# Attention's softmax division moved from each head pair to each finished token tile

## The chip, the core and the metric

The kernel runs on one core of one Trainium2 chip. A core has five engines that run their own queues in order and meet through semaphores: TensorE (PE, matmuls; PEld is its weight load), VectorE (DVE), ScalarE (ACT), GpSimd (POOL) and SyncE (SP, which here only issues DMAs). The metric is the time of one execution on the device in microseconds; lower is better.

## The reference, cut to what matters

Three stages follow each other: attention with a top-32 mask, a dense feed-forward layer ("MoE1" below) and a layer of 8 experts with top-1 routing.

```
scores = (1 / sqrt(64)) * q @ k^T              # 4 batches, 8 heads, 576 tokens, 64 per head
mask   = scores >= (32nd largest of the row)
attn   = exp(where(mask, scores, -1e9) - max)
attn   = attn / (sum(attn) + 1e-9)             # the division that the change moves
x      = (attn @ v), heads side by side         # 2304 tokens x 512
h = x @ w_in ; g = relu(h) + log1p(exp(-|h|)) ; x2 = g @ w_out      # MoE1, 2048 wide
out    = expert of argmax(x2 @ w_gate): relu(x2 @ w1[e]) @ w2[e], times its gate weight
```

## The kernel before

Attention works on groups. A group is two "tiles" of 128 query rows x 576 keys; there are 72 groups, and 80 products with the values, since the two heads of a pair share one product tile. For one group PE computes scores into PSUM (`emit_qk`, L387), ACT copies them to SBUF (L395), and DVE finds the 32 largest of each row: pairwise maxima and minima (L423 to L439), rounds of MAX8 and MATCH_REPLACE8 (L429 to L447). ACT takes the exponential (L436), DVE the mask (L458, with the product on POOL in L459, or L455 for both in one), ACT and POOL split the result into two float16 parts (L463 to L465), a DMA of SP's queue transposes it (L467, `pT`).

Three groups later (`LAG`) `emit_av` multiplies by the values. The value tile carries a column of ones, so column 64 of the PSUM tile `m` holds the sum of the exponentials (L482, L484). `m` has one buffer. Then, for each of the 80 head pairs, DVE forms the reciprocal of the two sums (L506, L508) and ACT writes each of the two heads, scaled by it, into the token tile `x` (L510). The next product cannot start before these two copies have read `m`.

A token tile (128 tokens x 512) is finished after four head pairs; there are 18. `unit_x` then splits it: ACT rounds it to float16 (`xh`, L529), POOL subtracts for the second part (L530), SP's queue transposes (L531, `xT`). One or two tiles make one of 10 units of MoE1; a unit is 16 steps, each of 12 matmuls with `w_in` (`layer1`, L569), four activations, an addition on POOL (L578) and, two steps later, the matmuls with `w_out` (`layer2`, L603; in the last two units L600). Then `route` writes the tile's rows and expert. In the first 300 us the weights of MoE1 are also decoded (L226 to L239). After attention and MoE1 comes the expert stage (`part_two`, L903 and L916 on PE).

What sets the order: the code emits groups, products and 1.7 steps of MoE1 per group with priorities (`A_SC`, `A_AV`, `AHEAD`), and a scheduler lays each engine's queue out from them and its own estimates. So an edit moves neighbours too. If a run's checks of magnitudes fail, a second, slower path (`flags is None`) does everything again; it is built but not executed here.

Of the kernel before, what the change touches and what calls it, by code (L numbers as in the profile page):

```python
# [8 lines left out]
F32 = mybir.dt.float32  # L9
# [4 lines left out]
AF = mybir.ActivationFunctionType  # L14
ALU = mybir.AluOpType
# [4 lines left out]
B, H, S, D = 4, 8, 576, 64  # L20
# [3 lines left out]
NP = H // 2  # L24
# [12 lines left out]
ESC = 1024.0  # L37
LN_ESC = 6.931471805599453
SCORE = 0.125
X_UP = 5  # L40
# [6 lines left out]
XB = 1  # L47
# [137 lines left out]
def part_one(tc, ctx, q, k, v, w_in, w_out, const, ident, before, ones, iota_e, reg_e, wg, ids,  # L185
             ohcum, done, early, table, rows, flags, sums, w_sums):
    nc = tc.nc
    late = []

    def pool(name, bufs, **kw):  # L190
        return ctx.enter_context(tc.tile_pool(name=name, bufs=bufs, **kw))
# [6 lines left out]
    xp = pool("xp", 1)  # L198
    wp = pool("wp", 1)
    sm = pool("sm", 4)  # L200
# [169 lines left out]
    sc_t, pt_t, o_t, x_t = {}, {}, {}, {}  # L370
# [98 lines left out]

    def x_tile(key):  # L470
        if key not in x_t:
            x_t[key] = xp.tile([128, NP, 2, D], F32, name=f"x{key[1]}", bufs=XB if isinstance(key[1], int) else 1)
        return x_t[key]

    def emit_av(m, kind):
        b, hp = pairs[m]
        v16, sc = pair[m][3:5]
        pT = pt_t.pop((m, kind))
        def products(o, pT, h):
            for r in range(R):  # L480
                c = r if r < 5 else r - 5
                nc.tensor.matmul(o[:, h, 0:D + 1], lhsT=pT(r), rhs=v16[:, h, c, 0:D + 1], start=r == 0, stop=r == R - 1)  # L482
                if r < 5:
                    nc.tensor.matmul(o[:, h, 0:D], lhsT=pT(r), rhs=v16[:, h, c, D + 2:], start=False, stop=False)  # L484

        def out_tile():
            return ps_m.tile([128, 512], F32, name="m")[:, :2 * D + 4].rearrange("p (h c) -> p h c", h=2)

        if kind == "tail":
            o = out_tile()  # L490
            p0 = 64 * (b % 2)
            for h in range(2):
                products(o[p0:p0 + 64], lambda r: pT[:, r, h * 64:h * 64 + 64], h)
            xt, ps_ = x_tile((b // 2, "tail%d" % (b // 2))), slice(p0, p0 + 64)
        else:
            t, h = kind
            if h == 0:
                o_t[m, t] = out_tile()
            o = o_t[m, t]
            products(o, lambda r: pT[:, r, :], h)  # L500
            if h == 0:
                return
            del o_t[m, t]
            xt, ps_ = x_tile((b, t)), slice(0, 128)
        rc = sm.tile([128, 2, 1], F32, name="rc")
        nc.vector.tensor_scalar(rc[ps_], o[ps_, :, D:D + 1], ESC * 1e-9,  # L506
                                2.0 ** -X_UP if flags is not None else sc[ps_, 2:3], op0=ALU.add, op1=ALU.mult)
        nc.vector.reciprocal(rc[ps_], rc[ps_])  # L508
        for h in range(2):
            nc.scalar.activation(xt[ps_, hp, h], o[ps_, h, 0:D], AF.Copy, scale=rc[ps_, h])  # L510


    def unit_x(tiles):
        n = 128 * len(tiles)
        up, dn, hs = 1.0, None, None
        if flags is None:
            bs = sorted({b for key, _ in tiles for b in ([key[0]] if isinstance(key[1], int) else [2 * key[0], 2 * key[0] + 1])})
            up = sm.tile([128, 1], F32, name="xup")
            nc.vector.tensor_reduce(up, v_up[:, bs[0]:bs[-1] + 1], op=ALU.min, axis=AX.X)
            dn = sm.tile([128, 1], F32, name="xdn")  # L520
            nc.vector.tensor_scalar(dn.bitcast(I32), up.bitcast(I32), -1.0, float(254 << 23), op0=ALU.mult, op1=ALU.add)
            hs = sm.tile([128, DFF // C], F32, name="hs")
        xT = xtp.tile([128, 2, 2, KD, 128], F16, name="xT")
        for i, (key, _) in enumerate(tiles):
            xv = x_t.pop(key).rearrange("p c h d -> p (c h d)")
            if flags is None:
                nc.scalar.activation(xv, xv, AF.Copy, scale=up)
            xh = x2p.tile([128, 2, DM], F16, name="xh", bufs=XHB)
            nc.scalar.activation(xh[:, 0], xv, AF.Copy)  # L529
            nc.gpsimd.tensor_tensor(out=xh[:, 1], in0=xv, in1=xh[:, 0], op=ALU.subtract)  # L530
            nc.sync.dma_start_transpose(out=xT[:, i].rearrange("p r c t -> p (r c) t"), in_=xh.rearrange("p r c -> p (r c)"))  # L531
        return xT, hs, dn

# [3 lines left out]
    def moe_step():  # L537

        if not cur and ready:
            cur.append(Unit(*ready.pop(0)))  # L540
        if cur:
            u = cur[0]
            if u.x is None:
                u.x = unit_x(u.tiles)
            layer1(u)
            behind.append((u, u.f))
            u.f += 1
            if u.f == KF - XAHEAD and ready:
                cur.append(Unit(*ready.pop(0)))
                cur[1].x = unit_x(cur[1].tiles)  # L550
            if u.f == KF:
                cur.pop(0)
        if behind and (not cur or len(behind) > GLAG):
            layer2(*behind.pop(0))
# [203 lines left out]
    for i in range(-1, n + LAG):  # L758
# [29 lines left out]
        if j >= 0:  # L788
            with tc.high_priority(offset=A_AV), ExitStack() as behind_scores:
                if i + 1 < n:  # L790

                    behind_scores.enter_context(tc.issue_after(last_qk[0].ins))
                for x in groups[j]:
                    emit_av(*x)
            for u in units.get(j, []):
                started += 1
                ready.append((u, started))
# [274 lines left out]
```

## Time and profile before

| what | value |
|---|---|
| median of 3 runs | 1112.18 us (1107.73 to 1112.3) |
| profiled execution | 1110.92 us |
| its span, first to last instruction | 1109.0 us |
| busy over the span | DVE 86%, PE 81%, ACT 72%, POOL 58% |

The span covers all but 1.92 us of the profiled execution. A share of busy time is a mean over stages: attention lasts to about 775 us (the last score copy starts at 757 us), what remains of MoE1 to about 870 us, and the expert stage to the end.

### The profile page before, as it was taken

To read this page: it belongs to the slowest core of one execution; us is meant where nothing else is said; L and a number is where in the kernel's file an instruction comes from. 1 tells how busy PE (TensorE), PEld (TensorE's weight loads), DVE (VectorE), ACT (ScalarE), POOL (GpSimd) and SP (SyncE) were. 2 spreads that over 40 slices of the span, in tenths; PEclk is the share of its full clock that TensorE was granted. 3 is DMA by queue.
4 is the path that set the end of the run, shared out by engine and by line. 5 is a ranking of instruction groups with operands and counts; after the bars stand their busy time and mean duration, and the time that the engine had idled before them with its cause. 6 is when DMAs were issued, how large, how long until landed. Compare 5 with 4: busy or idle time off the path is not lost.

```text
span 1109.0 us, 22601 instructions
## 1 busy us (share of the span) xinstructions
PE 896.1 (81%) x7146; PEld 646.9 (58%) x7146; DVE 948.9 (86%) x2985; ACT 799.2 (72%) x1898; POOL 638.3 (58%) x731
## 2 busy tenths in 40 slices
PE   1133257865987888899989999999999999999995
PEld 0012144543654555566556566656678889999994
DVE  4999999999978789999999999999646797777774
ACT  5767678886757778877888787777678755555553
POOL 3888798887556667766777766756434111221111
PEclk9975568997998899999999999999999999999998
DMA  8896777886467688635766764444701386576660
GB/s 195 193 204 155 179 172 169 175 203 118 75 108 115 127 125 162 128 74 96 139 137 125 110 104 73 93 66 74 207 25 30 98 244 211 202 242 239 217 230 23
DMA packets 295862, 157.00 MB, mean 142 GB/s; under 512 B 257524, under 2 KB 257652, under 8 KB 295732
## 3 DMA queue, kind: packets, MB, share of 16 engines
q1 hardware_dynamic: 292116, 145.73, 59.5%
q0 software_dynamic: 3616, 9.72, 2.5%
q8 instruction: 58, 0.95, 0.4%
q14 instruction: 72, 0.59, 0.2%
HBM read 77.89 MB, written 11.11 MB: 80 GB/s over the span
## 4 chain that ended last, share of the span: by engine, by line
DVE 33%; PE 33%; DMA 11%; issue 8%; ACT 7%; POOL 6%; SPq 1%; POOLq 0%; ACTq 0%; DVEq 0%
PE h L903 8%; PE y L916 8%; DVE mx L447 7%; DVE wk L443 6%; PE h L569 5%; PE y L603 4%; DMA pT<-p 4%; DVE mk L458 3%; PE y L600 2%; DVE xr L231 2%; DVE e L455 2%; DVE wk L439 2%; POOL p L465 1%; DVE mx L429 1%; DVE gt L424 1%
## 5 line engine op out<-in xcount | busy, mean ns | idle before, releaser
L603 PE MATMUL y<-w_out_s,g 128*128 128x512 f32 x480 | 240.1, 626 | 25.9 <-POOL g L578 25.9
L569 PE MATMUL h<-xT,w_in_s 128*128 128x256 f16 (+1 forms) x1920 | 228.9, 270 | 22.9 <-DMA xT<-xh 9.2
L569 PEld LDWEIGHTS <-w_in_s 128*128 128x128 f16 x1920 | 174.6, 101 | 95.3 <-issue 59.8
L387 PE MATMUL s<-kt,q 128*128 128x512 f16 (+7 forms) x640 | 99.0, 318 | 128.2 <-DVE wk L439 89.6
L447 DVE MAX8 mx<-wk 128x8 f32<-128x144 f32 (+2 forms) x432 | 199.9, 496 | 0.2
L578 POOL TENSOR_TENSOR g<-g,sa 128x256 f32<-128x256 f32 (+1 forms) x160 | 119.4, 749 | 100.1 <-ACT sa L577 91.8
L465 POOL TENSOR_TENSOR p<-e,p 128x512 f16<-128x512 f32 x144 | 168.9, 1173 | 0.0
L463 ACT ACTIVATE p<-e 128x576 f16<-128x576 f32 x144 | 98.3, 684 | 68.7 <-DMA pT<-p 30.4
L387 PEld LDWEIGHTS <-q 128*128 128x128 f16 (+1 forms) x640 | 45.0, 108 | 172.1 <-DVE wk L439 70.8
L443 DVE MATCH_REPLACE8 wk<-mx,wk 128x144 f32<-128x144 f32 (+1 forms) x432 | 144.8, 341 | 0.1
L603 PEld LDWEIGHTS y<-w_out_s,g 128*128 128x128 f32 x480 | 85.5, 198 | 95.5 <-issue 61.1
L459 POOL TENSOR_TENSOR e<-e,mk 128x576 f32<-128x576 f32 x84 | 109.8, 1309 | 46.8 <-DVE mk L458 23.9
L883 POOL DMA_INDIRECT out_dram<-ot,idx x19 | 19.5, 1028 | 176.5 <-DVE ot L882 173.7
L903 PEld LDWEIGHTS h<-xT,wf 128*128 128x128 f32 x864 | 111.7, 191 | 5.4 <-ACT wf L864 0.2
L903 PE MATMUL h<-xT,wf 128*128 128x256 f32 x864 | 113.8, 283 | 0.0
L916 PE MATMUL y<-wf,hT 128*128 128x512 f32 x432 | 113.0, 399 | 0.0
L436 ACT ACTIVATE e<-s,bias 128x576 f32<-128x576 f32 x144 | 105.9, 771 | 1.2
L482 PE MATMUL m<-v,pT 128*128 128x65 f16 (+1 forms) x1440 | 93.1, 201 | 10.8 <-ACT x L510 9.3
L482 PEld LDWEIGHTS <-pT 128*128 128x128 f16 (+1 forms) x1440 | 86.3, 106 | 15.5 <-issue 11.4
L395 ACT ACTIVATE s<-s 128x1152 f32<-128x1152 f32 x72 | 80.6, 1119 | 5.3 <-PE s L387 5.2
L916 PEld LDWEIGHTS y<-wf,hT 128*128 128x128 f32 x432 | 76.7, 189 | 13.1
L484 PE MATMUL m<-v,pT 128*128 128x64 f16 (+1 forms) x800 | 76.3, 200 | 0.0
(198 smaller groups left out, 1903.7 us busy)
## 6 DMA issues: line engine op xcount, KB each, us to landing
w1r<-in_moe_w_dram SPq DMA_DIRECT2D x20, 1024.0 KB, 5.1
w2r<-in_moe_w_dram SPq DMA_DIRECT2D x20, 1024.0 KB, 6.5
w<-in_moe_w_in_dram SPq DMA_DIRECT2D x16, 512.0 KB, 5.6
w<-in_moe_w_out_dram SPq DMA_DIRECT2D x16, 512.0 KB, 4.1
rows<-xr SPq DMA_DIRECT2D x37, 128.2 KB, 2.6
qn<-in_q_dram SPq DMA_DIRECT2D x16, 288.0 KB, 3.3
kn<-in_k_dram SPq DMA_DIRECT2D x16, 288.0 KB, 3.2
vn<-in_v_dram SPq DMA_DIRECT2D x16, 288.0 KB, 3.1
```

What stands on the lines that cost most here:

```text
L387: last_qk[0] = nc.tensor.matmul(ps[p0:p1, base + k0 * D:base + k1 * D], lhsT=lhs, rhs=kt[:, k0:k1, cs], start=first, stop=not first)
L436: nc.scalar.activation(e[i], s[i], AF.Exp, bias=bt[:, i], scale=SCORE if flags is not None else sc[i][:, 3:4])
L443: nc.vector.match_replace(out=to, in_to_replace=mx[:, i, 8 * j:8 * j + 8], in_values=src[i], imm_value=NEG)
L447: nc.vector.max(out=mx[:, i, 8 * j + 8:8 * j + 16], in_=src[i])
L459: nc.gpsimd.tensor_tensor(out=e[i], in0=e[i], in1=mk, op=ALU.mult)
L465: nc.gpsimd.tensor_tensor(out=p16[:, S + D:], in0=e[i][:, 0:S - D], in1=p16[:, 0:S - D], op=ALU.subtract)
L482: nc.tensor.matmul(o[:, h, 0:D + 1], lhsT=pT(r), rhs=v16[:, h, c, 0:D + 1], start=r == 0, stop=r == R - 1)
L569: nc.tensor.matmul(hps[:, :n], lhsT=w_in_s[:, c, j, p, o:o + 128], rhs=xT[:, 0:len(u.tiles), r, c, :], start=m == 0, stop=m == 3 * KD - 1)
L578: nc.gpsimd.tensor_tensor(out=g, in0=g, in1=a[:, :n], op=ALU.add)
L603: nc.tensor.matmul(u.y[i], lhsT=g[:, cs], rhs=w_out_s[:, f, :], start=f == 0, stop=f == KF - 1)
L903: nc.tensor.matmul(h, lhsT=w1f[:, a, c, :], rhs=xT[:, b, c, :], start=n == 0, stop=n == 3 * KD - 1)
L916: nc.tensor.matmul(y[i], lhsT=hT[g][:, a, i * 128:i * 128 + 128], rhs=w2f[:, b, :], start=g == 0 and n == 0, stop=g == KF2 - 1 and n == 2)
```

## The change

In the path that runs, `emit_av` no longer divides. One ACT copy per head pair takes both heads and their sums (2 x 65 columns) from `m` into `x`, whose tile now has 65 columns per head. `unit_x` divides once per token tile: DVE adds the small constant and forms 8 reciprocals, POOL multiplies the 128 x 8 x 64 values in place by them, and only then follow the rounding on ACT and the subtraction on POOL. All else is unchanged in the source.

```diff
-            x_t[key] = xp.tile([128, NP, 2, D], F32, name=f"x{key[1]}", bufs=XB if isinstance(key[1], int) else 1)
+            x_t[key] = xp.tile([128, H, D + 1], F32, name=f"x{key[1]}", bufs=XB if isinstance(key[1], int) else 1)
...
+        if flags is not None:
+            nc.scalar.activation(xt[ps_, 2 * hp:2 * hp + 2], o[ps_, :, 0:D + 1], AF.Copy)
+            return
         rc = sm.tile([128, 2, 1], F32, name="rc")
-        nc.vector.tensor_scalar(rc[ps_], o[ps_, :, D:D + 1], ESC * 1e-9,
-                                2.0 ** -X_UP if flags is not None else sc[ps_, 2:3], op0=ALU.add, op1=ALU.mult)
+        nc.vector.tensor_scalar(rc[ps_], o[ps_, :, D:D + 1], ESC * 1e-9, sc[ps_, 2:3], op0=ALU.add, op1=ALU.mult)
         nc.vector.reciprocal(rc[ps_], rc[ps_])
         for h in range(2):
-            nc.scalar.activation(xt[ps_, hp, h], o[ps_, h, 0:D], AF.Copy, scale=rc[ps_, h])
+            nc.scalar.activation(xt[ps_, 2 * hp + h, 0:D], o[ps_, h, 0:D], AF.Copy, scale=rc[ps_, h])
...
-            xv = x_t.pop(key).rearrange("p c h d -> p (c h d)")
+            xs = x_t.pop(key)
+            xv = xs[:, :, 0:D]
             if flags is None:
                 nc.scalar.activation(xv, xv, AF.Copy, scale=up)
+            else:
+                rc = sm.tile([128, H, 1], F32, name="rc")
+                nc.vector.tensor_scalar(rc, xs[:, :, D:D + 1], ESC * 1e-9, 2.0 ** -X_UP, op0=ALU.add, op1=ALU.mult)
+                nc.vector.reciprocal(rc, rc)
+                nc.gpsimd.tensor_tensor(out=xv, in0=xv, in1=rc.to_broadcast([128, H, D]), op=ALU.mult)
             xh = x2p.tile([128, 2, DM], F16, name="xh", bufs=XHB)
-            nc.scalar.activation(xh[:, 0], xv, AF.Copy)
-            nc.gpsimd.tensor_tensor(out=xh[:, 1], in0=xv, in1=xh[:, 0], op=ALU.subtract)
+            hi, lo = [xh[:, i].rearrange("p (h d) -> p h d", d=D) for i in range(2)]
+            nc.scalar.activation(hi, xv, AF.Copy)
+            nc.gpsimd.tensor_tensor(out=lo, in0=xv, in1=hi, op=ALU.subtract)
```

The scheduler lays the queues out anew. In the kernel after, the tile's reciprocals are L534 and L535, its product L536, the rounding L539, the subtraction L540, the copy of a head pair L507, and the later lines are 10 higher (L578 becomes L588).

DVE before, around a group's end early in attention (`rc` holds the two reciprocals of a head pair):

```order
L443 MATCH_REPLACE wk<-mx,wk 128x288 x2
L506 TENSOR_SCALAR rc<-m 128x2
L447 MAX mx<-wk 128x8
L423 TENSOR_TENSOR s<-s 128x288
L447 MAX mx<-wk 128x8
L508 RECIPROCAL rc<-rc 128x2
L458 TENSOR_SCALAR mk<-s,mx 128x576
L424 TENSOR_TENSOR gt<-s 128x288
```

DVE after, around the group's end where the first token tile is divided:

```order
L447 MAX mx<-wk 128x8
L423 TENSOR_TENSOR s<-s 128x288
L447 MAX mx<-wk 128x8
L534 TENSOR_SCALAR rc<-x_758 128x8
L458 TENSOR_SCALAR mk<-s,mx 128x576
L424 TENSOR_TENSOR gt<-s 128x288
L458 TENSOR_SCALAR mk<-s,mx 128x576
L535 RECIPROCAL rc<-rc 128x8
L425 TENSOR_TENSOR wk<-s,gt 128x2x144
```

The pair of small operations of every head pair is gone; such a pair stands once per token tile.

POOL before, at the first token tile (`x_758`; `p_...` are the split attention rows, `t` and `w_out_s` decoded weights, `st` a split query or key):

```order
L232 TENSOR_TENSOR t<-xr,w 128x512
L346 TENSOR_TENSOR st<-qn,st 128x9x64
L530 TENSOR_TENSOR xh<-x_758,xh 128x512
L459 TENSOR_TENSOR e<-e,mk 128x576
L239 TENSOR_TENSOR w_in_s<-t,w_in_s 128x512
L459 TENSOR_TENSOR e<-e,mk 128x576
```

POOL after, at the same tile:

```order
L536 TENSOR_TENSOR x_758<-x_758,rc 128x8x64
L464 TENSOR_TENSOR p_1382<-e,p_1382 128x64
L465 TENSOR_TENSOR p_1382<-e,p_1382 128x512
L232 TENSOR_TENSOR t<-xr,w 128x512
L346 TENSOR_TENSOR st<-kn,st 128x9x64
L464 TENSOR_TENSOR p_1388<-e,p_1388 128x64
L465 TENSOR_TENSOR p_1388<-e,p_1388 128x512
L540 TENSOR_TENSOR xh<-x_758,xh 128x512
```

The product stands where the subtraction stood, and the subtraction stands seven rows behind it. On PE the first matmuls of MoE1 follow 180 instead of 162 matmuls of L482 (one group later), and before the last score 1428 instead of 1440 matmuls of L569 and 218 instead of 220 of L603 are queued: one step of MoE1 fewer.

ACT before, at the third token tile (L463 splits attention rows, L573 and L575 are MoE1):

```order
L510 ACTIVATE x_1795<-m,rc 128x64 x2
L463 ACTIVATE p_2816<-e 128x576
L315 ACTIVATE junk,sums<-vn 128x576
L573 ACTIVATE sa<-h 128x256
L575 ACTIVATE g<-h 128x256
L529 ACTIVATE xh<-x_1795 128x512
L573 ACTIVATE sa<-h 128x256
```

ACT after, at the third token tile:

```order
L463 ACTIVATE p_2752<-e 128x576
L539 ACTIVATE xh<-x_1767 128x512
L507 ACTIVATE x_1896<-m 128x130
L395 ACTIVATE s<-s 128x1152
L436 ACTIVATE e<-s,bias 128x576
```

The rounding now needs POOL's product, and the next group's score copy (L395) and an exponential (L436) stand behind it here.

## Rows read from the trace of the kernel before

**Rows 1.** The page: busy time of each engine, share of the span, instructions.

```profile
PE 896.1 (81%) x7146; PEld 646.9 (58%) x7146; DVE 948.9 (86%) x2985; ACT 799.2 (72%) x1898; POOL 638.3 (58%) x731
```

**Rows 2.** Stretches: length, then busy us of PE, PEld, DVE, ACT, POOL; clock, DMA.

```profile
0.00:150.00 150.00, 38.14 (x328) 22.66 (x328) 133.95 (x364) 102.75 (x200) 113.84 (x120) 0.73 0.81 184
150.00:300.00 150.00, 112.58 (x927) 70.98 (x928) 149.09 (x450) 123.66 (x287) 126.27 (x132) 0.87 0.72 153
300.00:450.00 150.00, 125.61 (x1015) 79.75 (x1014) 126.10 (x442) 108.54 (x266) 97.20 (x115) 0.94 0.73 125
450.00:757.00 307.00, 285.57 (x2566) 189.28 (x2564) 295.15 (x1073) 247.10 (x626) 215.34 (x267) 0.98 0.58 103
757.00:870.00 113.00, 109.20 (x883) 81.49 (x881) 73.20 (x282) 87.36 (x269) 49.14 (x65) 1.00 0.33 81
```

**Rows 3.** The same stretches for line L506 alone: its DVE time and count.

```profile
0.00:150.00 150.00, 1.14 (x8) 0.73 0.81 184
150.00:300.00 150.00, 2.15 (x15) 0.87 0.72 153
```

**Rows 4.** Groups: line, engine, operation, count; busy us, mean ns; idle before.

```profile
L506 DVE TENSOR_SCALAR rc<-m 128x2 f32<-128x2 f32 (+1 forms) x80 | 11.8, 147 | 14.1 <-PE m L482 13.9
L508 DVE RECIPROCAL rc<-rc 128x2 f32<-128x2 f32 (+1 forms) x80 | 12.1, 152 | 0.4
L510 ACT ACTIVATE x<-m,rc 128x64 f32<-128x64 f32 x128 | 32.9, 313 | 15.1 <-DVE rc L508 14.1 <-DVE sf L981 1.0
```

**Rows 5.** Timeline of DVE, two group starts: start us, duration us.

```profile
337.63 0.51 DVE L458 TENSOR_SCALAR mk<-s,mx 128x576 f16<-128x576 f32 x1
338.06 0.15 DVE L506 TENSOR_SCALAR rc<-m 128x2 f32<-128x2 f32 x1
338.13 0.45 DVE L423 TENSOR_TENSOR s<-s 128x288 f32<-128x288 f32 x1
338.50 0.15 DVE L508 RECIPROCAL rc<-rc 128x2 f32<-128x2 f32 x1
338.62 0.46 DVE L424 TENSOR_TENSOR gt<-s 128x288 f32<-128x288 f32 x1
...
360.79 0.47 DVE L423 TENSOR_TENSOR s<-s 128x288 f32<-128x288 f32 x1 [0.85 <-ACT s L395]
361.29 0.46 DVE L424 TENSOR_TENSOR gt<-s 128x288 f32<-128x288 f32 x1
```

**Rows 6.** Timeline of DVE and ACT around two waits for a product.

```profile
372.13 0.16 DVE L506 TENSOR_SCALAR rc<-m 128x2 f32<-128x2 f32 x1 [5.34 <-PE m L482]
372.26 1.12 ACT L395 ACTIVATE s<-s 128x1152 f32<-128x1152 f32 x1
374.31 0.46 DVE L423 TENSOR_TENSOR s<-s 128x288 f32<-128x288 f32 x1
...
791.81 0.16 DVE L506 TENSOR_SCALAR rc<-m 128x2 f32<-128x2 f32 x1 [5.47 <-PE m L482]
```

**Rows 7.** Lines by themselves: durations ns as least/median/most.

```profile
L573 ACT ACTIVATE sa<-h x160: 253/368/440, 159.9 to 866.3; 128x256 f32<-128x256 f32 x128, 128x128 f32<-128x128 f32 x32
L458 DVE TENSOR_SCALAR mk<-s,mx x84: 492/514/1603, 29.2 to 772.3; 128x576 f16<-128x576 f32 x84
```

**Rows 8.** Waits over the span: total us, times, longest us.

```profile
DVE s L423 <- ACT s L395: 13.3, 11, 5.7
```

**Rows 9.** Groups of POOL and PE that price the added work, columns as in Rows 4.

```profile
L465 POOL TENSOR_TENSOR p<-e,p 128x512 f16<-128x512 f32 x144 | 168.9, 1173 | 0.0
L232 POOL TENSOR_TENSOR t<-xr,w 128x512 int32<-128x512 int32 x16 | 22.6, 1414 | 16.0 <-ACT xr L226 9.0 <-DVE xr L231 4.6 <-ACT e L436 1.6
L569 PE MATMUL h<-xT,w_in_s 128*128 128x256 f16 (+1 forms) x1920 | 228.9, 270 | 22.9 <-DMA xT<-xh 9.2 <-ACT g L575 8.8 <-ACT w_in_s L238 2.3
L603 PE MATMUL y<-w_out_s,g 128*128 128x512 f32 x480 | 240.1, 626 | 25.9 <-POOL g L578 25.9
```

**Rows 10.** Timeline of ACT: the score copy before the group at 338.13.

```profile
335.39 1.11 ACT L395 ACTIVATE s<-s 128x1152 f32<-128x1152 f32 x1
```

## The prediction

> **What bounds the kernel now.** I read the page's busy times first, then the stretches, then single groups and places. Over the whole span DVE is busiest with 948.9 us, but no engine fills it [rows 1], so the answer lies in the stages. In the stretches [rows 2] the reader should compare DVE with PE: from 150 to 300 us DVE is busy 149.1 of 150 us and PE only 112.6; from 300 to 450 us neither is full (126.1 and 125.6), the two wait for each other and for transposes; from 450 to 757 us DVE has 295.2 and PE 285.6 of 307; from 757 us on PE has 109.2 of 113. So attention is bound by DVE, with PE close behind in its second half, and what follows the last score copy at 757 us is bound by PE. A microsecond that DVE saves in attention moves the end by up to one, as long as PE, with 21 us free from 450 to 757, follows, and as long as no step of MoE1 slides behind the last score.
>
> **The change part by part.** The sum is made against the profiled execution, 1110.9 us, which is 1.3 us under the median of the three runs, 1112.2.
>
> Removed from DVE: 80 x 2 operations for `rc`. By their durations, 147 and 152 ns, they are 11.8 + 12.1 = 23.9 us [rows 4]. But consecutive DVE operations overlap at their ends, so what one costs its queue is the distance from its start to the next start: L506 starts at 338.06 and L423 behind it at 338.13, 0.07 us [rows 5]. 160 x 0.07 = 11.2 us. Some cost nothing even so: between L423 and L424 there are 0.49 us with L508 between them (338.13 to 338.62) and 0.50 us without (360.79 to 361.29), since L424 is held anyhow [rows 5]. I take one in seven as hidden in this way, an estimate: 9.6 us. Added to DVE are 18 x 2 operations on 8 elements, not seen before; by the same distance 36 x 0.07 = 2.5 us, by the durations 36 x 0.15 = 5.4. I take 2.5, since they stand among the same neighbours. Net -7.1 us. From 300 to 450 us DVE has 24 us free, so I take half of that stretch's part off: **-6.5 us**. Ends: 0 and 23.9 - 2.5 = 21.4.
>
> Waits that go: DVE stood 13.9 us before L506 until PE had finished the product [rows 4]. 5.5 of them are the last product at 791.8 us, where attention is over and PE sets the pace [rows 6]; 8.4 us lie in attention. Much of it returns: at 372.13 DVE had waited 5.34 us, but the next group's scores were copied only by 372.26 + 1.12 = 373.38, and L423 started at 374.31 [rows 6]. Without the wait L423 could start 0.9 us earlier, not 5.3. A product that is late shows that PE is late, and then the scores are late too. I take a third: **-2.8 us**, with ends 0 and 8.4.
>
> ACT: two copies per head pair of 313 ns [rows 4] become one of 130 columns. A PSUM copy of 128 columns took 253 ns at the least and one of 256 a median of 368 [rows 7], so about 0.26 us: 160 x 0.31 - 80 x 0.26 is some 29 us less duration. ACT is not the bound in attention (247.1 of 307 us in its second half [rows 2]), so most of this is free time. It pays where DVE waits for a score copy, 11 times [rows 8]; a shorter copy ahead gives each at most 0.3 us. I take **-1 us**, ends 0 and 3.
>
> POOL: 18 products of 128 x 512. Operations of this size took 1.17 us in float and 1.41 in integers [rows 9]; I take 1.2, since floats are what is multiplied here: 21.6 us (21.1 to 25.4). POOL has 24 us free from 150 to 300 us and 92 from 450 to 757 [rows 2], so it costs nothing by itself. If that cover were gone, all 21.6 would count.
>
> The chain to `xT` gets longer by two DVE operations and the product. The order shows more than that: seven POOL rows stand between the product and the subtraction of the first tile, PE's first matmuls of MoE1 come one group later, and one step of MoE1 moves behind the last score. There PE is full, so its price is that of a step: 228.9 / 160 = 1.4 us for L569 and, at four records per step of two tiles, 240.1 / 120 = 2.0 us for L603 [rows 9]: **+3.4 us**. PE also waited 9.2 us for `xT` before L569 [rows 9]; with a longer chain I add **+1 us** (0 to 3). The last tile's chain lies beside the steps of the unit before it and is taken as free; if it weren't, it would cost the product, 1.2 us. SP's queue gets no new DMA, but a transpose of `xT` that waits holds the `pT` behind it; that is in the +1.
>
> Sum: -6.5 - 2.8 - 1 + 3.4 + 1 = -5.9, so 1110.9 - 5.9 = **1105 us**.
>
> **The rivals.** *Saved DVE time is not passed on* (chance 0.33). Only up to 300 us DVE is alone at its limit; later PE, at 93%, and the transposes set the pace in turn. Then only the pairs before 300 us count: 8 + 15 = 23 of 80 [rows 3], 46 x 0.07 x 6/7 = 2.8 us less 0.5 for the four tiles divided by then, and the step of MoE1 costs 3.4 all the same: 1110.9 - 2.3 + 3.4 = 1112 us. For it speaks PE's load, against it that DVE is still busier than PE from 450 to 757 us.
>
> *ACT stands behind POOL* (0.15), on the slower side. The rounding L539 must wait for a product that queues behind the split attention rows on POOL, and ACT's next score copy stands behind it. A wait as long as one L465 and the product, 1.17 + 1.2 = 2.4 us, at each of 18 tiles is 43 us of ACT. DVE feels what exceeds its lead: a score copy ended at 335.39 + 1.11 = 336.50 [rows 10] and was needed at 338.13, 1.6 us later [rows 5]. So 18 x 0.8 = 14 us arrive: 1119 us. It eats the gain when the mean wait passes 1.6 + 5.9 / 18 = 1.9 us. For it speaks the third tile, where only the copy of a head pair stands between L539 and L395; against it that at most tiles the order leaves one or two other split rows on ACT between.
>
> *Each product holds a DVE operation up* (0.04). L458, with a median of 514 ns, took up to 1603 [rows 7]; if each product blocked DVE for its whole time, 18 x 1.2 = 21.6 us would come on top: 1127 us. The median says that most L458 run freely beside a POOL that is busy 84% from 150 to 300 us, so I give it little. [...]
>
> *The operations cost their full duration and the waits stay away* (0.06): 23.9 - 2.5 + 8.4 - 3.4 = 26 us, 1085 us. The start distances speak against it [rows 5].
>
> **How the numbers follow.** The forecast, 1105, has 0.42 and its own range of 1100 to 1109. A measurement of this kernel can tell about 0.5% from no change, 5.6 us, so faster is below 1106.6 and slower above 1117.7. The forecast's range lies mostly below 1106.6 (0.38 of its 0.42); with the last rival faster has 0.44. No change has 0.33 + 0.04 = 0.37, slower 0.15 + 0.04 = 0.19. The range runs from 1092, which takes in the full 11.2 us and the full 8.4 of waits, to 1121 behind the rival on ACT; outside are the rivals of 1127 and 1085 and part of the one on ACT, under 2 in 10.
>
> **What would show it.** Right: DVE's count falls by 124 and its busy time in attention by 7 to 18 us (the page adds overlaps in part); no wait of DVE for a product; the last score copy near 748 us; PE still full behind it. The step that slid: L569 before the last score fewer by 12. [...] I would be wrong if the new order, which differs in nearly every place, shifts a transpose or a decoded weight by several microseconds; nothing in the trace of before can price that.

## The result and the profile after

| | before | after |
|---|---|---|
| time, us, median | 1110.2 (1107.7 to 1112.3) | 1121.4 (1119.1 to 1123.9) |
| ratio | | 1.0102, 95% interval 1.0067 to 1.0137 |
| profiled execution, its span, us | 1110.9, 1109.0 | 1121.2, 1119.1 |

The change made the kernel 1.0% slower, 11 us; forecast were 1105 us, 6 us faster, with a range of 1092 to 1121. (The kernel before has four runs here; the three known ahead of the prediction had the median of 1112.2.) On the chips of the experiments the kernel before itself takes 1115 to 1122 us, so each experiment is given as a ratio to the kernel before on its own chip, as recorded (which is not exactly the quotient of the medians). No trace of the unchanged kernel before was taken on those chips: where a trace of an experiment is set beside the trace of before or after, a difference of chips is in it too. How large it can be shows in the kernel after, five of whose traces have the same order on every engine up to 780 us (after and experiments 1, 5, 13 and 14): DVE is busy from 953.4 to 962.2 us in them, and the last mask of the softmax starts between 772.0 and 777.3 us.

The page of after, busy time of each engine, against [rows 1]:

```profile
PE 889.8 (80%) x7146; PEld 644.2 (58%) x7146; DVE 959.5 (86%) x2861; ACT 784.3 (70%) x1818; POOL 653.7 (58%) x749
```

DVE has 124 instructions fewer, as forecast, and is busy 10.6 us longer. The stretches of after, columns as in [rows 2]:

```profile
0.00:150.00 150.00, 37.61 (x328) 22.22 (x328) 134.48 (x348) 101.07 (x194) 114.78 (x120) 0.80 0.80 182
150.00:300.00 150.00, 102.35 (x878) 65.76 (x879) 149.97 (x410) 117.57 (x263) 127.88 (x132) 0.89 0.72 153
300.00:450.00 150.00, 130.61 (x1121) 84.08 (x1120) 134.89 (x456) 113.29 (x266) 105.08 (x128) 0.97 0.79 132
450.00:757.00 307.00, 278.23 (x2475) 182.52 (x2473) 293.96 (x984) 232.59 (x576) 215.90 (x267) 0.98 0.63 100
757.00:870.00 113.00, 106.46 (x845) 79.84 (x843) 67.78 (x263) 81.10 (x236) 49.74 (x65) 0.97 0.37 80
```

From 150 to 300 us DVE now has no free time at all (149.97 of 150) and does 40 instructions fewer than before; PE does 7 us less from 450 to 757 and 3 us less behind it. Where the 10 us of span come in is read from two lines: the last mask of the softmax (the last start of L458, 772.3 before [rows 7]) and the last step of MoE1 (the last start of L573, 866.3 before [rows 7], L583 now). In after:

```profile
L458 DVE TENSOR_SCALAR mk<-s,mx x84: 495/510/2359, 29.6 to 772.0; 128x576 f16<-128x576 f32 x84
...
L583 ACT ACTIVATE sa<-h x160: 255/368/427, 171.5 to 876.6; 128x256 f32<-128x256 f32 x128, 128x128 f32<-128x128 f32 x32
```

So attention ends where it did (-0.3 us), and the stretch behind it, "the tail" below, takes 104.6 us for 94.0 (+10.6). What follows the last step takes 242.5 us in after and 242.7 in before. In attention two things cancel, as the stretch up to 757 us shows (columns as in [rows 2]), first before, then after:

```profile
0.00:757.00 757.00, 561.90 (x4833) 362.66 (x4834) 704.29 (x2324) 582.05 (x1376) 552.66 (x632) 0.90 0.68 133
0.00:757.00 757.00, 548.79 (x4797) 354.57 (x4798) 713.29 (x2195) 564.52 (x1297) 563.65 (x644) 0.92 0.71 133
```

DVE has 129 operations fewer there and is busy 9.0 us longer, and its idle time falls by the same 9.0 us, from 52.7 to 43.7. Two questions follow: why does DVE get busier with 124 operations fewer, and why is the tail longer?

**DVE.** Groups of after: the new operations L534 (add and scale) and L535, then small operations of MoE1's routing and the softmax that the change doesn't touch:

```profile
L534 DVE TENSOR_SCALAR rc<-x 128x8 f32<-128x8 f32 x16 | 10.9, 682 | 7.1 <-ACT x L507 7.1
...
L671 DVE TENSOR_TENSOR ohcum<-ohcum,oh 128x8 f32<-128x8 f32 x18 | 10.6, 587 | 0.0
L450 DVE TENSOR_TENSOR flags<-mx 128x16 f32<-128x16 f32 x18 | 9.8, 543 | 0.0
L664 DVE TENSOR_SCALAR oh<-iota_e,nm 128x8 f32<-128x8 f32 x18 | 9.6, 536 | 0.1
...
L535 DVE RECIPROCAL rc<-rc 128x8 f32<-128x8 f32 x18 | 3.2, 183 | 0.0
...
L662 DVE RECIPROCAL xr<-gs 128x1 f32<-128x1 f32 x18 | 2.7, 150 | 0.1
```

These tensor-by-scalar and two-tensor operations of 8 or 16 elements read only SBUF and take 536 to 682 ns on the mean, about three to four times as long as the reciprocals (150 and 183 ns), which read SBUF too. The old L506 of [rows 4], which read PSUM, took 147 ns. What they wait for shows on the timeline of DVE and POOL, at two of the new L534:

```profile
527.27 0.94 POOL L588 TENSOR_TENSOR g<-g,sa 128x256 f32<-128x256 f32 x1
528.18 1.27 POOL L346 TENSOR_TENSOR st<-kn,st 128x576 f16<-128x576 f32 x1
...
528.65 3.15 DVE L534 TENSOR_SCALAR rc<-x 128x8 f32<-128x8 f32 x1
529.42 1.11 POOL L540 TENSOR_TENSOR xh<-x,xh 128x512 f16<-128x512 f32 x1
530.50 1.27 POOL L459 TENSOR_TENSOR e<-e,mk 128x576 f32<-128x576 f32 x1
531.72 0.44 DVE L424 TENSOR_TENSOR gt<-s 128x288 f32<-128x288 f32 x1
...
708.82 1.28 POOL L459 TENSOR_TENSOR e<-e,mk 128x576 f32<-128x576 f32 x1 [1.31 <-DVE mk L458]
...
709.03 1.10 DVE L534 TENSOR_SCALAR rc<-x 128x8 f32<-128x8 f32 x1
...
710.05 0.45 DVE L424 TENSOR_TENSOR gt<-s 128x288 f32<-128x288 f32 x1
```

At 709.03 it starts beside a running POOL operation and ends at 710.13, 0.03 us after that one's end (710.10). At 528.65 it ends at 531.80, 0.03 us after the third POOL operation in a row (531.77). Nine of the 18 took over 0.5 us, and all nine end within 0.04 us behind the end of a POOL operation; where POOL stood idle beside it, at 138.2, 516.0 and 790.8 us, it took 0.14 to 0.17 us. The reciprocals took 0.15 to 0.19 us wherever they stand. So nine of the L534 waited here for the end of a GpSimd operation: 0.14 to 0.17 us free and up to 3.15 us held. How long the same 16 `rc<-x` operations are held differs from one execution to the next: their mean is 461 ns in experiment 1, 502 in experiment 5 and 606 in experiment 14, with the same order up to 780 us.

**The tail.** TensorE's timeline in after, from a MoE1 step to the first half of the last product and a step behind it (other rows of the product left out):

```profile
776.18 1.15 PE L579 MATMUL h<-xT,w_in_s 128*128 128x256 f16 x9
777.16 0.29 PE L701 MATMUL h<-ohcum,ones 128*128 128x8 f32 x2
783.87 0.24 PE L483 MATMUL m<-v,pT 128*128 128x65 f16 x1 [6.42 <-DMA pT<-p]
...
784.62 3.76 PE L613 MATMUL y<-w_out_s,g 128*128 128x512 f32 x4
788.18 1.62 PE L579 MATMUL h<-xT,w_in_s 128*128 128x256 f16 x12
```

Between the product before and the last one stand only these nine matmuls of a step and the two small ones of L701 in TensorE's queue, so it waits 6.42 us for the transposed probabilities. Behind the wait the granted clock is 0.50 from 784 to 788 us and 0.63 on the mean from 784 to 790 us:

```profile
784.00:790.00 6.00, 6.00 (x42) 3.56 (x41) 0.00 (x0) 0.11 (x1) 0.00 (x0) 0.63 0.77 268
```

Four L613 take 3.76 us there, where the kernel before needs 1.88 at 782.02 (clock 1.00 from 780 to 784), and after itself needs 1.88 again at 791.37 (clock 1.00 from 791 to 794). Before, MoE1 steps fill the same place: the longest wait there is 2.4 us (at 778.05). In the program's order 129 of the 160 MoE1 steps stand ahead of the last product in the kernel before, and 125 in after. By the last mask 124 steps had run before and 122 now; TensorE's busy time from there to the copy behind the last step, 3.6 us past the tail, is 94.0 us before and 101.0 after, its idle time 3.5 and 7.1.

### The profile page after: what moved, and what is told of

The parts are those of the page before. It is cut to its first block, busy times and chain, and to the rows that moved or that the text cites. A ratio compares the mean times of both kernels' runs of the same rounds, so it can differ in the third digit from the quotient of the medians.

```text
span 1119.1 us, 22324 instructions
## 1 busy us (share of the span) xinstructions
PE 889.8 (80%) x7146; PEld 644.2 (58%) x7146; DVE 959.5 (86%) x2861; ACT 784.3 (70%) x1818; POOL 653.7 (58%) x749
## 4 chain that ended last, share of the span: by engine, by line
DVE 35%; PE 32%; DMA 11%; ACT 7%; issue 7%; POOL 4%; SPq 2%; POOLq 0%; ACTq 0%; DVEq 0%
PE h L913 9%; PE y L926 9%; DVE mx L447 7%; DVE wk L443 7%; PE h L579 4%; DMA pT<-p 4%; DVE mk L458 3%; PE y L613 3%; DVE wk L439 3%; DVE e L455 3%; PE y L610 2%; DVE xr L231 2%; DVE wk L425 2%; DVE mx L429 2%; DVE gt L424 2%
## 5 line engine op out<-in xcount | busy, mean ns | idle before, releaser
L613 PE MATMUL y<-w_out_s,g 128*128 128x512 f32 x480 | 235.8, 617 | 18.8 <-POOL g L588 18.7
L579 PE MATMUL h<-xT,w_in_s 128*128 128x256 f16 (+1 forms) x1920 | 220.2, 265 | 19.6 <-ACT g L585 17.2
L387 PE MATMUL s<-kt,q 128*128 128x512 f16 (+7 forms) x640 | 101.3, 322 | 158.1 <-DVE wk L439 117.4
L579 PEld LDWEIGHTS <-w_in_s 128*128 128x128 f16 x1920 | 171.6, 99 | 83.4 <-issue 65.1
L588 POOL TENSOR_TENSOR g<-g,sa 128x256 f32<-128x256 f32 (+1 forms) x160 | 116.6, 732 | 102.6 <-ACT sa L587 90.5
L463 ACT ACTIVATE p<-e 128x576 f16<-128x576 f32 x144 | 98.2, 682 | 75.4 <-DMA pT<-p 28.4
L613 PEld LDWEIGHTS y<-w_out_s,g 128*128 128x128 f32 x480 | 85.0, 197 | 89.0 <-issue 61.8
L436 ACT ACTIVATE e<-s,bias 128x576 f32<-128x576 f32 x144 | 106.7, 768 | 2.4 <-POOL p L465 0.9
L483 PEld LDWEIGHTS <-pT 128*128 128x128 f16 (+1 forms) x1440 | 87.0, 106 | 22.9 <-issue 12.2
L395 ACT ACTIVATE s<-s 128x1152 f32<-128x1152 f32 x72 | 80.7, 1121 | 6.8 <-PE s L387 6.5
```

The costliest lines, as they stand in the source:

```text
L387: last_qk[0] = nc.tensor.matmul(ps[p0:p1, base + k0 * D:base + k1 * D], lhsT=lhs, rhs=kt[:, k0:k1, cs], start=first, stop=not first)
L436: nc.scalar.activation(e[i], s[i], AF.Exp, bias=bt[:, i], scale=SCORE if flags is not None else sc[i][:, 3:4])
L579: nc.tensor.matmul(hps[:, :n], lhsT=w_in_s[:, c, j, p, o:o + 128], rhs=xT[:, 0:len(u.tiles), r, c, :], start=m == 0, stop=m == 3 * KD - 1)
L588: nc.gpsimd.tensor_tensor(out=g, in0=g, in1=a[:, :n], op=ALU.add)
L613: nc.tensor.matmul(u.y[i], lhsT=g[:, cs], rhs=w_out_s[:, f, :], start=f == 0, stop=f == KF - 1)
```

## The experiments

Two causes were to be told apart: what holds DVE (the "scale", L534, above all) and the planned order of the tail. The first four ran on one chip. Where an expectation counts the stretch behind the last softmax, it counts to that copy, 3.6 us more than the tail here (108.1 us in after).

**1. Two steps ahead of the last product.** In the changed kernel 18 steps are emitted earlier, and the last product is put behind them, which leaves 126 steps ahead of it.

```diff
...
+            if j == n - 1:
+                some_work(18)
             with tc.high_priority(offset=A_AV), ExitStack() as behind_scores:
+                if j == n - 1:
+                    behind_scores.enter_context(tc.issue_after(last_moe[0].ins))
```

> The kernel after, with two steps of MoE1 moved ahead of the last product with the values in PE's queue; the order before that point is the same. Theory A (the lost time is in the tail): the changed kernel's PE stood empty 6.4 us before the last product and then ran about 4 us at half clock; both go, the time falls by 8 to 11 us to about 1111 us, with the wait for pT under 1 us. Theory B (the loss is spread over attention, and the tail only shows it): the work moved ahead is missing behind it, the time stays within 3 us of 1121.

Measured 1121.8 us, ratio 1.0012 (0.9982 to 1.0043), for 1.0102 of the changed kernel on another chip: as theory A has it. TensorE is busy 37.8 of the 40 us from 760 to 800, for 33.6 in after: the hole is gone.

**2. The scale on ScalarE.** One edit; the reciprocal stays on DVE.

```diff
-                nc.vector.tensor_scalar(rc, xs[:, :, D:D + 1], ESC * 1e-9, 2.0 ** -X_UP, op0=ALU.add, op1=ALU.mult)
+                nc.scalar.activation(rc, xs[:, :, D:D + 1], AF.Copy, scale=2.0 ** -X_UP, bias=ESC * 1e-9 * 2.0 ** -X_UP)
```

> The kernel after, with the scaling and small constant of the token tile's sums (one DVE operation per tile, 0.58 us of DVE's queue each) done by ACT; the reciprocal stays on DVE. [...] Theory B (DVE is held up there by whatever stands in the queue): the neighbours take over the delay, less than 3 us of DVE's time goes.

Measured 1120.0 us, ratio 0.9989 (0.9963 to 1.0015), 1.1% under the changed kernel's 1.0102 on another chip, some 12 us. DVE's busy time is 942.4 us for 959.5, a fall of 17.1 where theory B had less than 3, and the last mask stands at 769.7. The tail keeps its hole (TensorE 32.8 of 40 us).

**3. Both.**

> Both edits of the two kernels above: sums scaled on ACT, and two steps of MoE1 ahead of the last product. [...] If only the tail counts: about 1111. If neither: 1121.

Measured 1113.9 us, ratio 0.9947 (0.9912 to 0.9983): faster than the kernel before, with all of the computation kept.

**4. Another order alone.** The kernel before with one planner's number changed (`A_PREP` 130 for 150), which moves some 5,900 rows of the order and no operation.

> The kernel before with one priority changed, that of the preparation of a head pair (130 for 150): no operation more or less, some 5900 rows of the five queues in another place. It prices what a new order alone does. If orders are worth little: 1110 within 3 us. If a new order alone can be worth the loss of the change: 5 us or more away from 1110, either way.

Measured 1118.7 us, ratio 0.9989 (0.9964 to 1.0014). This one other order costs nothing, so a new order alone need not; it doesn't show that none would. It is not without effect on DVE: L455 takes 960 ns on the mean here, for 896 before, and `oh` 456 for 385, without any operation added.

**5 to 8** ran on a second chip.

**5. The changed kernel again.**

> The changed kernel as it stands, on the chip of its neighbours here, to read their ratios against. If the loss belongs to the program, the ratio to the kernel before is 1.007 to 1.014 again, and the 20 us window from 780 shows the last product of TensorE waiting some 6 us for its transposed probabilities. If the loss depends on the chip, the ratio is near 1.00.

Measured 1129.1 us, ratio 1.0088 (1.0053 to 1.0124): the loss belongs to the program. TensorE waits 7.1 us for the last transposed probabilities.

**6. No scale, two steps ahead.** The factor goes into the column of ones, and the added 1e-9 is left out.

```diff
-        nc.gpsimd.memset(vs[:, :, D:D + 2], 1.0)
+        nc.gpsimd.memset(vs[:, :, D:D + 2], 1.0 if flags is None else 2.0 ** -X_UP)
...
-                nc.vector.tensor_scalar(rc, xs[:, :, D:D + 1], ESC * 1e-9, 2.0 ** -X_UP, op0=ALU.add, op1=ALU.mult)
-                nc.vector.reciprocal(rc, rc)
+                nc.vector.reciprocal(rc, xs[:, :, D:D + 1])
```

> The column of ones beside the values is written as 1/32, so the sum of the exponentials arrives already scaled and the 16 operations that scale it on VectorE are gone (only the reciprocal stays; the added 1e-9 is left out, which is below the last bit of a sum of at least 1024); with it two steps of the first MoE layer are put between the last two products, as in the tail experiment. Theory 'held-up scale and tail order': the scale's 10.9 us leave VectorE's busy time (959.5 to some 948) without the ACT operation that took their place in the third experiment, so the ratio is at or below that one's, 0.991 to 0.996. Rival 'the moved scale on ScalarE only gave another order by chance': the ratio is that of the tail experiment alone, 0.999 to 1.004.

Measured 1114.2 us, ratio 0.9961 (0.9937 to 0.9985), at the upper end of what the first theory expected (0.996); DVE 947.4 us, last mask at 766.0.

**7. The kernel before with a product per tile.**

```diff
...
+                nc.gpsimd.tensor_tensor(out=x4, in0=x4, in1=ones[:, 0:DM // D].rearrange("p (a o) -> p a o", o=1).to_broadcast([128, DM // D, D]), op=ALU.mult)
             xh = x2p.tile([128, 2, DM], F16, name="xh", bufs=XHB)
```

> The kernel before, with one thing added: each token tile is multiplied in place on GpSimd by a broadcast column of ones, between the last copy into the tile and its rounding; the division stays per head pair. Output unchanged. Theory 'GpSimd's product holds up VectorE's operations in SBUF': VectorE's busy time grows by 5 to 10 us with no operation added, seen in the small sums of the routing (400 to over 500 ns) and the flags (391 to over 450 ns), and the time by 4 to 8 us. Rival 'the product is covered': VectorE's busy time stays within 2 us and the time within 2 us.

Measured 1139.0 us, ratio 1.0185 (1.0144 to 1.0226): much more than either theory. DVE's busy time grows by 10.8 us to 959.7 without one operation more, as the first theory has it; `oh` goes from 385 to 610 ns, `flags` from 391 to 476, L455 from 896 to 976 (but L455 has 960 in experiment 4, without a product). The rest of the loss is longer waits, with the last mask at 790.6: L455 waits 16.7 us for ScalarE's exponentials. Why these come late wasn't found.

**8. The kernel before with the scale per tile**, its result unread.

```diff
...
+                nc.vector.tensor_scalar(ex, x4[:, :, D - 1:D], ESC * 1e-9, 2.0 ** -X_UP, op0=ALU.add, op1=ALU.mult)
```

> The kernel before, with one thing added: one VectorE operation per token tile of the shape of the new scale (128x8 out of SBUF with a stride of 64, two scalars), whose result nobody reads. Theory 'an operation out of SBUF stands held up there whatever the product does': it takes 500 ns or more on the mean, VectorE's busy time grows by 8 to 11 us, and the time by 3 to 8 us. Rival 'it is held up only because GpSimd's product and the tile's copies stand beside it in the changed kernel': 100 to 200 ns on the mean, VectorE +2 to +3 us, time within 2 us.

Measured 1130.3 us, ratio 1.0115 (1.0075 to 1.0155). Its group:

```profile
L531 DVE TENSOR_SCALAR ext<-x 128x8 f32<-128x8 f32 x16 | 6.9, 429 | 10.2 <-ACT x L510 10.1
```

And the line by itself, durations as least/median/most:

```profile
L531 DVE TENSOR_SCALAR ext<-x x16: 147/381/1056, 137.9 to 803.0; 128x8 f32<-128x8 f32 x16
```

It is held without a product on GpSimd, though less than expected (429 ns on the mean for 500 or more), while L506, which reads PSUM, keeps its 147 ns in the same trace; and DVE waits 10.1 us for the tile's last copy before it. DVE's busy time grows by 6.0 us and the time by 1.2%, some 13 us, which the busy time alone doesn't explain. Up to the last mask, 12.2 us later than in the trace of before, DVE's idle time is 6.3 us longer; since L423 and L506 wait 4.6 and 5.2 us less beside the new wait of 10.1, where this comes from is open.

**9 to 12**, on a third chip, were to undo the order wholly.

**9. Steps ahead in the last eight groups.** In the changed kernel each of the last eight groups' products is put behind as many MoE1 steps as in the kernel before.

```diff
...
+    ahead = [117, 119, 120, 122, 124, 126, 127, 129]
...
+            want = ahead[j - n] if j >= n - len(ahead) else 0
+            while steps[0] < want and (ready or cur):
+                some_work(1)
...
+                if want:
+                    behind_scores.enter_context(tc.issue_after(last_moe[0].ins))
```

> The changed kernel, all its operations kept; only TensorE's order in the last eight groups is set: as many steps of the first MoE layer stand ahead of a group's products as in the kernel before (117, 119, 120, 122, 124, 126, 127 and 129 of 160, where the changed kernel has 114, 116, 118, 120, 120, 122, 123 and 125 ahead of the last ones). Theory 'the tail's loss is the planned order: four steps of some 2.6 us behind the last product': the stretch from the last softmax to the last step falls from 108 us to 97 to 101, and the ratio to the kernel before from 1.009 to 0.998 to 1.002. Rival 'the steps are late because the engines that feed them are late, and the order only records it': the attention ends later by what the steps ahead of it take, the last step ends where it did, ratio 1.006 to 1.012.

Measured 1125.5 us, ratio 1.0041 (1.0015 to 1.0067), between the two theories: the last mask at 778.6 us and 102.3 us behind it (last step at 880.9), less than in after but well over what was expected. Against the changed kernel's 1.0065 to 1.0102 on three other chips some 3 to 7 us come back; attention ends 2.4 us later than in experiment 5, which is no more than chips differ by.

**10. Steps behind, in the kernel before.**

```diff
...
+        behind_g = [g for g, cap in zip((-4, -3, -2, -1), (120, 122, 123, 125)) if cap <= steps[0]]
+        if behind_g:
+            held.enter_context(tc.issue_after(last_av[groups[behind_g[-1]][-1]].ins))
...
```

> The reverse in the kernel before, all its operations kept: steps of the first MoE layer held behind the products of the last four groups, so that 120, 122, 123 and 125 stand ahead of them as in the changed kernel. Theory 'planned order': the ratio is 1.006 to 1.010, the last softmax within 2 us of where it was and the stretch behind it 105 to 108 us instead of 98. Rival 'the order only records it': the products and the softmax end earlier by what the steps no longer take, ratio 0.998 to 1.002.

Measured 1125.3 us, ratio 1.0042 (1.0015 to 1.0069): the order of the tail alone costs the kernel before some 5 us, somewhat less than expected. The last mask stands at 776.2, the last step at 880.9, a tail of 104.7 us as in after. Up to the last step TensorE is idle only 2.6 us in this tail, for 6.6 in after: this price is that of steps that come late, without a hole.

**11. No scale, the changed kernel's own order.**

> The changed kernel with the scale's 16 operations gone, as in the experiment with the column of 1/32 (the added 1e-9 left out again), and its own order at the end, which has 125 steps ahead of the last product. Theory 'two causes that add: some 10 us on VectorE and some 8 us of order': last softmax 8 to 10 us earlier than in the changed kernel, the stretch behind it still 108 us, ratio 0.998 to 1.002. Rival 'the order is the only cause': ratio 1.007 to 1.012.

Measured 1121.2 us, ratio 1.0006 (0.9979 to 1.0034), as two causes have it; last mask 767.7, tail 106.3 us.

**12. No scale, steps ahead in the last eight groups.**

> Both: the scale's operations gone and the steps ahead of the last eight groups as in the kernel before. Theory 'two causes that add': last softmax as in the one without the scale, the stretch behind it 97 to 101 us, ratio 0.987 to 0.993, faster than the kernel before. Rival 'each repair only moves the wait': ratio 0.996 to 1.000, as with two steps moved.

Measured 1120.0 us, ratio 0.9997 (0.9973 to 1.0022): not the 0.987 to 0.993 expected, but as its rival has it. In this order DVE is busy 962.8 us, as long as with the scale (L455, moved to L456 here, has 1010 ns on the mean), and the tail is 104.6 us. So with the scale gone the repair of the order over eight groups gives nothing (0.9997 for 1.0006). What the last product's place alone is worth is seen next.

**13 to 16: four corners on one chip.** The scale kept or gone, the last product where the planner put it or two steps later.

> First of four corners taken on one chip (scale operation kept or gone, planned end kept or two steps moved ahead of the last product): the changed kernel itself, both kept. By the runs on three chips so far: ratio to the kernel before 1.007 to 1.012. If its share depends on the chip, it lies outside.

> Scale kept, two steps moved ahead of the last product. Two causes that add: 4 to 6 us under the first corner, ratio 1.002 to 1.007, all of it behind the last softmax (TensorE's idle time there 3 to 4 us for 7 to 8). Order alone is the cause: ratio at or under 0.997.

> Scale gone (the added 1e-9 with it), planned end kept. Two causes that add: 7 to 11 us under the first corner, ratio 0.998 to 1.003, all of it ahead of the last softmax. Scale alone is the cause: ratio at or under 0.996.

> Scale gone and two steps moved. Two causes that add: the sum of the two differences, 11 to 17 us under the first corner, ratio 0.993 to 0.998. One cause seen twice: no better than the better of the two single corners.

| | planned place | two steps later |
|---|---|---|
| scale kept | 1127.0 us, 1.0065 (1.0039 to 1.0091) | 1120.8 us, 1.0001 (0.9975 to 1.0028) |
| scale gone | 1122.1 us, 1.0012 (0.9985 to 1.0039) | 1113.1 us, 0.9941 (0.9917 to 0.9966) |

The place is worth 6.2 us with the scale and 9.0 without, the scale 5.0 and 7.7; together they are worth 14.0, for 11.2 of the two singly (the surplus of 2.8 is not clear of the noise): there are two causes, and they add. Neither alone gives what the rivals expected of it (at or under 0.997 for the place, 0.996 for the scale). Taking the scale out also lays out attention anew, from 136 us on; against that order being the cause speak experiment 4 and that two ways of taking it off DVE, with different orders (0.9989 in experiment 2; 1.0006 and 1.0012 in 11 and 15), give nearly the same. TensorE's longest wait behind the last mask (total us, times, longest us), scale kept, planned place:

```profile
PE m L483 <- DMA pT<-p: 6.8, 1, 6.8
```

Two steps later:

```profile
PE y L613 <- POOL g L588: 2.2, 1, 2.2
```

Last mask and last step with scale and planned place:

```profile
L458 DVE TENSOR_SCALAR mk<-s,mx x84: 493/514/2356, 28.0 to 772.1; 128x576 f16<-128x576 f32 x84
...
L583 ACT ACTIVATE sa<-h x160: 253/367/424, 169.4 to 878.6; 128x256 f32<-128x256 f32 x128, 128x128 f32<-128x128 f32 x32
```

With neither:

```profile
L458 DVE TENSOR_SCALAR mk<-s,mx x84: 466/512/2209, 29.2 to 767.6; 128x576 f16<-128x576 f32 x84
...
L582 ACT ACTIVATE sa<-h x160: 254/367/442, 171.6 to 866.5; 128x256 f32<-128x256 f32 x128, 128x128 f32<-128x128 f32 x32
```

The tail is 106.5 us in the first and 98.9 in the second. So the place shows in the tail: 106.5 and 100.4 us with the scale, 106.9 and 98.9 without. The scale's share does not show in the two traces of the planned place, which are of executions of nearly the same time (1124.2 and 1123.8 us, while the medians are 1127.0 and 1122.1): DVE is busy 7.7 us less up to the last mask without it and idle 7.2 longer, and the mask comes at 772.1 and 771.6. A single trace moves by more than that, so the scale's share is read better over all: six profiles with it on DVE have the last mask at 775.3 on the mean (772.0 to 778.6), five with it gone and the product on GpSimd at 768.5 (766.0 to 771.6), 6.8 us.

**17. The product on VectorE**, added to the fourth corner.

```diff
-                nc.gpsimd.tensor_tensor(out=xv, in0=xv, in1=rc.to_broadcast([128, H, D]), op=ALU.mult)
+                nc.vector.tensor_tensor(out=xv, in0=xv, in1=rc.to_broadcast([128, H, D]), op=ALU.mult)
```

> The corner with the scale gone and the two steps moved, with one thing more: the tile's product runs on VectorE instead of GpSimd (18 of 128x512). The planner orders the end anew, 128 steps ahead of the last product for 126. Theory 'the product on GpSimd holds VectorE up by about its own size': VectorE gains 18 x 0.7 = 12.6 us of operations and loses as much in shorter hold-ups, busy time 948 to 956 us, ratio within 0.003 of that corner's 0.994 to 0.996. Rival 'the product is covered on GpSimd and holds nothing up': VectorE's busy time 960 to 966 us, last softmax 6 to 12 us later, ratio 1.000 to 1.006.

Measured 1136.9 us, ratio 1.0183 (1.0153 to 1.0213): both theories missed the time. Groups of DVE in it:

```profile
L455 DVE SCALAR_TENSOR_TENSOR e<-s,mx,e 128x576 f32<-128x576 f32 x60 | 53.9, 898 | 8.1 <-ACT e L436 7.3 <-POOL p L465 0.9
...
L535 DVE TENSOR_TENSOR x<-x,rc 128x512 f32<-128x512 f32 x16 | 17.4, 1084 | 0.0
...
L450 DVE TENSOR_TENSOR flags<-mx 128x16 f32<-128x16 f32 x18 | 7.2, 398 | 0.0
...
L670 DVE TENSOR_TENSOR ohcum<-ohcum,oh 128x8 f32<-128x8 f32 x18 | 5.2, 289 | 0.0
```

With the product off GpSimd, `flags` falls from 650 ns in the fourth corner to 398, `ohcum` from 489 to 289 and L455 from 983 to 898, some 13 us together: that agrees with a hold-up by GpSimd's product, though the order is another here too. But the product is itself held on DVE (1084 ns on the mean, 676 at the least), the busy time rises to 958.4 us, and DVE's waits for score copies (L423 on L395) are 28.4 us, for 16.7 in the fourth corner. The last mask comes at 791.7. As in experiment 7, the time grows by more than DVE's busy time, and why is open.

## Why the prediction was wrong, step by step

In the traces the forecast is 16 us off: attention ends 0.3 us earlier for some 9 forecast, and the tail grows by 10.6 us for 3.4.

*What bounds the kernel* held in kind, not in measure: with the scale taken off DVE attention ends earlier on the mean (6.8 us, experiments 13 to 16). But busy time is not the price of an operation. DVE's busy time falls by 9.0 us at the planned place (962.2 to 953.2) and the time by 5.0, with two steps moved by 1.7 (953.4 to 951.7) and 7.7; a single trace can't resolve it, since 962.2 and 953.4 are two executions with the same order up to 780 us. The last score copy starts at 758.3 us, not near 748.

*DVE, -6.5 us: failed, in the added part.* The removed 160 operations were sized at 9.6 us; by the distance from start to next start, less idle time, they stood for 14.1 us in the trace of before, so that side was, if anything, too small. The 36 added ones were sized at 2.5 ("since they stand among the same neighbours"), for 5.4 by durations. They last 14.1 us in the rows above (10.9 + 3.2), and by the same distances those in attention hold DVE's queue for 11.6, nearly all of it the scale: 2.5 us are saved, not 7.1. The neighbours are the same; the operand isn't. L506 read PSUM (147 ns on the mean), L534 reads SBUF (682 ns), beside a GpSimd that is busy 85% of the time from 150 to 300 us. The trace of before had the right row for it, a tensor-by-scalar of 128x8 out of SBUF in the routing:

```profile
L654 DVE TENSOR_SCALAR oh<-iota_e,nm 128x8 f32<-128x8 f32 x18 | 6.9, 385 | 0.1
```

18 of these and 18 reciprocals at 150 ns give 9.6 us, as much as was put down for what left. On top the untouched operations L450, L455, L664 and L671 take 12.5 us longer than before, 3.6 of it L455. Experiments 7 and 17 agree with products on GpSimd doing that; but L455 and `oh` also rose in experiment 4 by a new order alone, so how much of it each does is open.

*Each product holds a DVE operation up* (0.04) was the nearest rival in its mechanism, and was given little for the median of L458. That median is still 510 ns; the hold-up shows on small operations, of which a median of a large one says nothing. It isn't the product alone either: experiment 8 has the scale held without it.

*Waits, -2.8*: too small by the trace. The 13.9 us before L506 are gone, L423's waits for scores rose from 13.3 [rows 8] to 20.4 us as the prediction expected in kind, and DVE's idle time up to 757 us fell from 52.7 to 43.7, more than the term's upper end of 8.4. That gain was eaten by the busier DVE.

*ACT, -1*: its busy time fell by 15 us; no run tells what of that reached the end.

*POOL, 0*: failed as a reading of cover. GpSimd's free time hid its own work, not what its work did to DVE: 10.8 us of busy time in experiment 7, a difference of chips and order included.

*The step of MoE1 behind the last score, +3.4: failed in its size and its mark.* Four steps moved behind the last product, not one behind the last score; two fewer had run by the last mask (5.4 us at 2.7 us a step in the tail), TensorE stood empty 3.6 us longer and ran at a lower clock behind it (0.63 on the mean from 784 to 790 us, for 1.00 before from 780 to 784). In sum the tail grew by 10.6 us. The order shows the four steps before any run. Not all of it need be the order: forced on the kernel before (experiment 10) it costs some 5 us, and moving the last product back brings 6 to 9 (13 to 16).

*ACT behind POOL* (0.15) did not come: ACT waited 1.5 us for a product, not 43. *Saved DVE time is not passed on* (0.33) described attention well (last mask 0.3 us earlier) for a wrong reason: there was no saved time to pass on. *xT*, +1, did not come: TensorE's waits for `xT` in L579 are 0.9 us, for 9.2 before in L569 [rows 9]; the rounding waited 3.2 us for the transposes, for 2.0 before.

Without the two missed terms the total comes out near the forecast: scale gone and the last product two steps later, the ratio is 0.9941 and 0.9961, 4 to 7 us faster than before, and the forecast was 6. With the scale on ScalarE (experiment 3), which keeps every term of the formula, it is 0.9947. That the total agrees is in part luck, since the terms don't: DVE's busy time in these three is 951.7, 947.4 and 943.2 us, for 948.9 in the trace of before, so a busy time some 7 us shorter is in none of them. Not settled is why a product added to GpSimd (experiment 7) or moved to DVE (17) costs attention about twice and over three times what DVE's busy time shows, and why fewer steps, 121 to 123 for 124, have run by the last mask in every version that has the product on GpSimd.

## What to carry to other kernels

Price a small VectorE operation by a row with the same operation and operand memories, not by one of the same size: here the scale out of SBUF beside a busy GpSimd took 0.43 us (experiment 8) to 0.68 us (after) on the mean, L506 out of PSUM 0.15, and the reciprocals 0.15 (before) to 0.18 (after). Before you move an operation from many small places to few late ones, count in the new order how much independent work stands ahead of the last link of the chain; four steps behind it cost the kernel before 5 us by themselves (experiment 10), nearly the 6 us that the change was to gain. A constant factor is best put where it costs nothing, here into the column of ones that makes the sums. And before a difference of a few microseconds between two traces is explained, see how far two traces of one kernel lie apart: 9 us of DVE's busy time here.

## What the runs showed of the hardware

One waiting VectorE operation let several GpSimd operations pass: the L534 at 528.65 us stood through the ends of two and ended with the third, 3.15 us for 8 elements a partition. Among the small operations beside it, those held were tensor-by-scalar and two-tensor operations of 8 or 16 elements with all inputs in SBUF (536 to 682 ns on the mean); a tensor-by-scalar of one element a partition (L661) took 146 ns on the mean, a reciprocal of 8 elements 0.19 us at most. After 6.4 us without a matmul TensorE's granted clock was 0.50 from 784 to 788 us and 1.00 from 791 to 794, and four L613 took 3.76 us, twice the 1.88 of the next four.
